# Windowed attention and a leaky-ReLU layer: the q and k casts of batches 4 to 7 go to GpSimd alone, and the list that orders the work counts transfers of later batches as landing later

## The chip, the cores and the metric

The kernel runs on one core of one Trainium2 chip. The metric is the device time of one execution in microseconds (us); the time before is the median of three runs. One further execution was recorded by the hardware profiler; all durations below come from that one. Engines are named as in the profile: PE is TensorE's matmul, PEld its weight load, DVE is VectorE, ACT is ScalarE, POOL is GpSimd, SP is SyncE, whose queue issues nearly all transfers.

## The reference

There are 8 batches of 8 heads with 576 positions of 64 numbers. Each query sees keys of a window only: heads 0 to 3 the last 32 positions, heads 4 to 7 every fourth of the last 128 ("dilated"). The result of attention, 4608 tokens of 512 numbers, goes through two matrices with a leaky ReLU between.

```python
scores = scale * np.matmul(q, k.transpose(0, 1, 3, 2))
rel = pos[:, None] - pos[None, :]
mask_plain = (rel >= 0) & (rel < window)                     # window 32
mask_dil = (rel >= 0) & (rel < window * dilation) & (rel % dilation == 0)   # dilation 4
attn = softmax of the scores under the head's mask
x = attn @ v, heads side by side                              # 4608 x 512
h = x @ w_in                                                  # 512 x 2048
out = np.maximum(0.01 * h, h) @ w_out                         # 2048 x 512
```

## The kernel before

**Two streams of work share the engines.** Attention is done batch by batch; within a batch it goes by pairs of heads, four visits in the order dilated, dilated, plain, plain. The layer is done in 12 chunks of 384 tokens, three for every two batches: `up` (L1012) is `w_in` times the attention's result `xt`, ACT applies the leaky ReLU and writes `gt` (L1023), and the products with `w_out` (L1065 and L1156) follow. From the fifth token tile on, four tiles are taken together in `group`, which replaces eight block products by seven (a Strassen scheme); the sums and differences this needs are DVE instructions at L1142, and the results are put together at L1185 (ACT or DVE) and L1193 (DVE).

**How q and k of batches 2 to 7 reach the scores.** For each half of a batch (two visits), SP issues four transfers of q and four of k into two `stg` buffers; there are four such buffers for this, so the two halves that follow each other use different ones. A cast from float32 to float16 takes one visit's q or k from `stg` to `nat` (three buffers): four casts of 128x576 per half, eight per batch, 48 in all. It shows as L287 on POOL and as L285 on ACT. DVE then transposes `nat` (L621, L636, L655); for the dilated heads POOL rearranges what DVE turned (L642, L649). The result is in `slots` (six of them), from which PE makes the scores (L949). ACT takes the exponential (L962), DVE multiplies by the mask (L965), PE sums and applies v (L955), ACT makes the reciprocal of the sum (L973, L976), DVE normalizes into `xt` (L984). v has its own casts on POOL (L287, `v_all<-vst`), four per batch.

**What sets the order.** Nothing is ordered on the chip: a list scheduler, `_Plan.run`, runs as Python while the program is built. Each task has costs on the engines that may do it, a latency, dependencies and a priority. The planner gives each engine its tasks in the order of its modelled start times, and where a task may run on several engines it takes the one that ends it soonest. On the chip every engine then works through its list in that order and waits at each instruction for what it needs. For a transfer the plan counts the time to issue it, its service time and then `1.1 + t.late`; `t.late` is `LATE` for the transfers of batches 2 to 7 and of the late masks, and less for those ahead:

```python
server = begin + t.service
t.done = server + 1.1 + t.late
```

The tasks that need the transfer are ready after `t.done` in the plan, and so are the loads that reuse the buffer when those tasks have ended. The number changes the order alone; no instruction waits for it on the chip. The modelled cost of a cast of n columns is `0.05 + n * 0.00102` us on POOL and `0.06 + n * 0.00087` us on ACT. Output stores stand in the same SP list as the loads.

Of the kernel before, what the change touches and what calls it, by code (L numbers as in the profile page):

```python
# [12 lines left out]
ALU = mybir.AluOpType  # L13

WIN = 32
AHEAD, LATE, HOLD = 5.0, 4.0, 5.0
WHEN = (-5.0, 15.0, 50.0, 77.0, 112.0, 138.0, 172.0, 200.0)
CON = -1484.5
AFTER = -1495.0
# [139 lines left out]
def kernel(  # L159
# [42 lines left out]
    def at(tl, p0, p1, off, *dims):  # L202

        row = tl.ap[0][0]
        return bass.AP(tensor=tl.tensor, offset=tl.offset + p0 * row + off,
                       ap=[[row, p1 - p0]] + [list(d) for d in dims])
# [73 lines left out]
    def cast(dst, src, n, deps, prio, engines=("POOL",)):  # L280
        cost = {"POOL": 0.05 + n * 0.00102, "DVE": 0.08 + n * 0.00056, "ACT": 0.06 + n * 0.00087}

        def fn(e):
            if e == "ACT":
                nc.scalar.copy(out=dst, in_=src)  # L285
            else:
                ENG[e].tensor_copy(out=dst, in_=src)  # L287
        return add(tuple((e, cost[e]) for e in engines), None, 0.2, deps, fn, prio, 0.0, "cast")
# [6 lines left out]
    def ring(name, n, users):  # L295

        r = rings.setdefault(name, [])
        waits = r[-n] if len(r) >= n else []
        r.append(users)
        return (len(r) - 1) % n, waits  # L300
# [43 lines left out]
    CENG = ("POOL", "DVE")  # L344
# [14 lines left out]
    def load_group(b, g, prio, prio_v):  # L359
# [3 lines left out]
        early = b < EARLY  # L363
# [64 lines left out]
        for j in range(2):  # L428
            nn, n_old = ring("NAT", NNAT, n_users := [])
            na, c_qk = nat[nn], []  # L430
            for o in range(2):
                st, s_users = stage[o]
                if early:
                    dst = at(na, 0, 128, o * 512, [D, 2], [128, 4], [1, D])
                    src = at(st, 0, 128, *((j * 512, [256, 2]) if first else (j * 256, [512, 2])), [D, 4], [1, D])
                    n = 512
                else:
                    dst, src, n = na[:, o * S:o * S + S], st[:, j * S:j * S + S], S
                c_qk.append(cast(dst, src, n, (loads[o][j:j + 1] if first else loads[o]) + n_old, prio,
                                 (("ACT",) if o else ("DVE",)) if first and dil and j == 0 else  # L440
                                 CENG if early else ("POOL", "ACT")))
                s_users.append(c_qk[-1])
            if not early:
                visits[b, 2 * g + j, 0] = (na, c_qk, n_users, vb[:, SLOT9 * j:SLOT9 * j + SLOT9],
                                           c_v, k_users)
                continue
            dn, d_old = ring("VD" if dil else "VP", NV, d_users := [])
            vt = (vd if dil else vp)[dn]
            n_v = 256 if dil else 384
            h_a, h_s = j * n_v, 2 * n_v  # L450
            n, w = n_v // D, 128 * (8 if dil else 6)
            c_v = [cast(at(vt, 0, 128, 0, [w, 2], [128, n], [1, D]),
                        at(vs, 0, 128, h_a, [h_s, 2], [D, n], [1, D]), 2 * n_v,
                        (lv if dil else lv[0] + lv[1]) + d_old, prio_v)]
            v_users += c_v
            seen_ones[b, 2 * g + j] = [t_ones["d" if dil else "p", dn]]
            kept[b, 2 * g + j] = vt, d_users
            visits[b, 2 * g + j, 0] = (na, c_qk, n_users, vt,
                                       c_v + ([t_one] if (b, 0) in TILED else
                                              [t_ones["d" if dil else "p", dn]]), d_users)  # L460
# [839 lines left out]
    def attend(b, part, first, step):  # L1300
        units = {None: (0, 1), 0: (0, 1), 1: (2,)}[part]
        if part is None and not late_mask:
            late_mask.append(load("SP", late_m, late_d, 128, 2 * NLATE, [], tick()))
        if part == 1:
            load_rest(b, ranks[b])
        for n, hp in enumerate((2, 3, 0, 1)):
            if part != 1 and n % 2 == 0:
                load_group(b, hp // 2, *(ranks[b, hp // 2, i] if b < EARLY else tick()
                                         for i in (0, 1)))
            got = turn(b, hp, part or 0, first + step * n)  # L1310
            for u in units:
                if part is None:
                    late_unit(b, hp, u, got, first + step * n)
                else:
                    unit(b, hp, part, u, got, first + step * n)
# [99 lines left out]
```

## Time and profile before

| what | value |
|---|---|
| time, median of 3 runs | 321.32 us (320.18 to 322.19) |
| the profiled execution: its time | 319.11 us |
| the profiled execution: its span, first to last instruction | 317.3 us |
| granted TensorE clock, mean | 0.999 |
| busy: PE, DVE, ACT, POOL | 297.9, 214.8, 202.9, 114.4 us |
| q and k casts 128x576 on POOL (L287) | 21, mean 727 ns |
| q and k casts 128x576 on ACT (L285) | 27, mean 674 ns |
| v casts 64x1152 on POOL (L287) | 24, mean 1235 ns |
| DVE transposes of `nat`, L621 and L636 | 24.0 and 17.4 us in all |
| POOL's waits for transfers of q and k / of v | 12.4 / 20.4 us |
| ACT's waits for transfers of q and k | 5.5 us |

The span is the time that the instructions cover; the 1.8 us between it and the execution's time lie around it. Busy times are sums over the whole span. An engine's wait is the idle time ahead of an instruction, put down to what came last; it costs time only where somebody waits for that engine in turn.

### The profile page before, as it was taken

The page shows a single profiled execution, that of the slowest core. Times are in us where ns is not written, and L with a number is a line of the kernel's source. Part 1 is how long each engine was busy: PE and PEld are TensorE (multiplying, and loading weights), DVE is VectorE, ACT ScalarE, POOL GpSimd, SP SyncE. Part 2 cuts the span into 40 slices and gives each one's busy share as a digit, 9 for nine tenths or more (in the row PEclk, how much of TensorE's full clock was granted, in tenths as well). Part 3 has the DMA queues.
Part 4 walks back from the last instruction along what each step waited for, and adds up shares of the span by engine and source line. Part 5 has one row for each costly group of instructions (what it writes and reads, how often), then busy time and mean ns, then how long its engine had stood idle before and what let it go on. Part 6 is the DMA issues. An engine that isn't in the chain of part 4 may idle for free.

```text
span 317.3 us, 7595 instructions
## 1 busy us (share of the span) xinstructions
PE 297.9 (94%) x2847; PEld 218.3 (69%) x2847; DVE 214.8 (68%) x422; ACT 202.9 (64%) x489; POOL 114.4 (36%) x156
## 2 busy tenths in 40 slices
PE   8868699899999999999997998999999999999985
PEld 3534365556988787787775876687877777767774
DVE  5786988975999989968868976886524341150172
ACT  3725464797898879587885876658565844454411
POOL 4479976259475166064508247120000000000000
PEclk9999999999999999999999999999999999999999
DMA  7999999689898996679859789612103010220223
GB/s 239 321 337 404 407 300 185 163 166 201 159 178 169 177 195 125 128 151 191 155 131 187 161 168 171 161 59 70 35 9 93 1 35 0 68 66 2 74 61 99
DMA packets 157300, 47.62 MB, mean 150 GB/s; under 512 B 137296, under 2 KB 154576, under 8 KB 157264
## 3 DMA queue, kind: packets, MB, share of 16 engines
q1 hardware_dynamic: 156688, 46.79, 62.2%
q8 instruction: 22, 0.36, 0.5%
q10 hardware_dynamic: 576, 0.35, 0.4%
q14 instruction: 14, 0.11, 0.1%
HBM read 37.68 MB, written 9.44 MB: 148 GB/s over the span
## 4 chain that ended last, share of the span: by engine, by line
PE 66%; DMA 7%; POOL 7%; SPq 5%; DVE 5%; ACT 4%; issue 4%; POOLq 0%; ACTq 0%; DVEq 0%
PE hps L1012 30%; PE fps L1156 19%; PE tp L1156 7%; SPq L277 5%; POOL w_in L287 4%; PE ops L955 3%; DMA wst<-in_moe_w_in_dram 3%; POOL v_all L287 2%; DMA stg<-in_q_dram 2%; PE fps L1065 2%; ACT gt L1023 2%; DVE slots L583 1%; DMA out_dram<-osb 1%; PE ops L1156 1%; DMA stg<-in_k_dram 1%
## 5 line engine op out<-in xcount | busy, mean ns | idle before, releaser
L1012 PE MATMUL hps<-xt,w_in 128*128 128x384 f16 (+1 forms) x812 | 146.7, 313 | 7.9 <-ACT gt L1023 3.3
L1023 ACT ACTIVATE gt<-hps 128x384 f16<-128x384 f32 (+1 forms) x203 | 93.3, 469 | 58.3 <-PE hps L1012 56.6
L1012 PEld LDWEIGHTS <-w_in 128*128 128x128 f16 x832 | 74.9, 98 | 43.8 <-issue 7.0
L1156 PEld LDWEIGHTS <-gt 128*128 128x128 f16 x768 | 73.1, 98 | 15.0 <-DVE gt L1142 2.0
L287 POOL CAST v_all<-vst 64x1152 f16<-64x1152 f32 (+3 forms) x36 | 39.8, 1111 | 26.1 <-DMA vst<-in_v_dram 20.4
L1156 PE MATMUL fps<-w_out,gt 128*128 128x256 f16 x368 | 47.5, 273 | 0.0
L984 DVE TENSOR_TENSOR xt<-ops,rc 128x288 f16<-128x288 f32 x48 | 26.8, 559 | 15.2 <-ACT rc L976 8.7
L965 DVE TENSOR_TENSOR ee<-ee,late_m 128x384 f16<-128x384 f16 (+1 forms) x48 | 22.8, 486 | 10.5 <-ACT ee L962 10.2
L1193 DVE TENSOR_TENSOR osb<-tp,stg 128x512 f32<-128x512 f32 x14 | 9.6, 687 | 27.1 <-ACT stg L1185 18.0
L621 DVE STREAM_TRANSPOSE slots<-nat 64x64 f16<-64x64 f16 (+1 forms) x48 | 24.0, 500 | 2.3 <-POOL nat L287 1.0
L287 POOL CAST nat<-stg 128x576 f16<-128x576 f32 (+1 forms) x24 | 17.0, 713 | 16.7 <-DMA stg<-in_q_dram 6.3
L285 ACT CAST nat<-stg 128x576 f16<-128x576 f32 (+1 forms) x28 | 18.5, 672 | 5.5 <-DMA stg<-in_q_dram 5.2
L1185 ACT COPY stg<-fps 128x512 f32<-128x512 f32 (+1 forms) x25 | 13.4, 535 | 12.9 <-PE fps L1156 12.7
L976 ACT ACTIVATE rc<-rc 128x288 f32<-128x288 f32 x48 | 21.3, 448 | 0.4
L642 POOL COPY slots<-turned 64x512 f16<-64x512 f16 x24 | 17.0, 710 | 10.3 <-DVE turned L636 9.5
L649 POOL COPY slots<-turned 128x576 f16<-128x576 f16 x12 | 8.7, 722 | 29.9 <-DVE turned L636 29.6
L636 DVE STREAM_TRANSPOSE turned<-nat 128x576 f16<-128x576 f16 (+1 forms) x24 | 17.4, 738 | 1.2 <-issue 0.9
L955 PEld LDWEIGHTS <-v_all 128*128 128x128 f16 x240 | 14.8, 98 | 3.4
L583 DVE COPY slots<-tp 64x128 f16<-64x128 f16 (+7 forms) x43 | 13.6, 333 | 4.5 <-PE tp L662 4.1
L1156 PE MATMUL fps<-wst,gt 128*128 128x256 f16 x128 | 16.4, 273 | 0.2 <-DVE gt L1142 0.2
L955 PE MATMUL ops<-ee,v_all 128*128 128x96 f16 (+2 forms) x240 | 16.4, 200 | 0.0
L1142 DVE TENSOR_TENSOR gt<-gt 128x1024 f16<-128x1024 f16 x21 | 15.0, 730 | 1.6 <-PE fps L1156 1.6
(113 smaller groups left out, 431.9 us busy)
## 6 DMA issues: line engine op xcount, KB each, us to landing
stg<-in_q_dram SPq DMA_DIRECT2D x48, 144.0 KB, 3.3
stg<-in_k_dram SPq DMA_DIRECT2D x48, 144.0 KB, 3.0
vst<-in_v_dram SPq DMA_DIRECT2D x12, 288.0 KB, 3.6
vst<-in_v_dram SPq DMA_DIRECT2D x24, 128.0 KB, 2.8
gt<-in_moe_w_in_dram SPq DMA_DIRECT2D x5, 512.0 KB, 8.0
xt<-in_moe_w_out_dram SPq DMA_DIRECT2D x3, 512.0 KB, 7.1
gt<-in_moe_w_out_dram SPq DMA_DIRECT2D x3, 512.0 KB
out_dram<-osb SPq DMA_DIRECT2D x12, 128.0 KB, 2.1
```

The lines of the kernel that those rows point to most:

```text
L285: nc.scalar.copy(out=dst, in_=src)
L287: ENG[e].tensor_copy(out=dst, in_=src)
L621: nc.vector.transpose(at(qb, p0, p0 + 64, p0 + c, *dims), na[p0:p0 + 64, S + c // 2:S + c // 2 + n])
L636: lambda e, xb=xb, o=o, n=n: nc.vector.transpose(xb[:, 0:n], na[:, o * S:o * S + n]),
L642: lambda e, xb=xb, p0=64 * h: ENG[e].tensor_copy(out=at(qb, p0, p0 + 64, p0, [128, 4], [512, 2], [1, 64]), in_=at(xb, p0, p0 + 64, 0, [1, ...
L955: nc.tensor.matmul(at(bk, 0, 128, o, *dims), stationary(s), et[:, c:c + n], start=i == 0, stop=i == len(parts) - 1, skip_group_check=True)
L965: lambda e: nc.vector.tensor_tensor(out=et[:, 0:w], in0=et[:, 0:w], in1=mk, op=ALU.mult), prio + 0.1)
L976: lambda e: nc.scalar.activation(out=rt[:, 0:NQ], in_=rt[:, 0:NQ], func=AF.Exp, scale=-1.0),
L984: lambda e: nc.vector.tensor_tensor(out=dst, in0=at(ot, 0, 128, 0, *src), in1=at(rt, 0, 128, 0, *src), op=ALU.mult), prio + 0.2)
L1012: nc.tensor.matmul(ht[:, 0:n], at(w_in, 0, 128, i * DFF + j // 2 * 256 + j % 2, [2, 128]), at(xt[m % 2], 0, 128, i * 1152 + x0 + x, [1, n] ...
L1023: lambda e: nc.scalar.activation(out=gt[c % NG][:, j * n_c + x:j * n_c + x + n], in_=ht[:, 0:n], func=AF.Prelu, alpha=0.01),
L1156: nc.tensor.matmul(bk[:, x:x + HN], tl[:, off + j * step:off + j * step + 128], rhs(j), start=first and x == 0 and j == 0, stop=j == HJ - ...
```

## The change

Two lines change. `LATE` goes from 4 to 7 us, and the q and k casts of batches 4 to 7 may run on POOL alone, where before the plan chose POOL or ACT for each. Batches 2 and 3 keep the choice, and batches 0 and 1 (`early`) are as they were. No instruction is added or taken away; the casts that ACT had for batches 4 to 7 become POOL's, and the whole list is made anew with the later landing times, so that the order may change on every engine from batch 2 on.

```diff
-AHEAD, LATE, HOLD = 5.0, 4.0, 5.0
+AHEAD, LATE, HOLD = 5.0, 7.0, 5.0
...
                 c_qk.append(cast(dst, src, n, (loads[o][j:j + 1] if first else loads[o]) + n_old, prio,
                                  (("ACT",) if o else ("DVE",)) if first and dil and j == 0 else
-                                 CENG if early else ("POOL", "ACT")))
+                                 CENG if early else ("POOL", "ACT") if b < 4 else ("POOL",)))
```

## The prediction

> **What bounds the kernel now.** I read the page's busy times and slices first, then the windows, PE's waits, and the timeline around each wait.
>
> ```profile
> PE 297.9 (94%) x2847; PEld 218.3 (69%) x2847; DVE 214.8 (68%) x422; ACT 202.9 (64%) x489; POOL 114.4 (36%) x156
> ...
> PE   8868699899999999999997998999999999999985
> ...
> POOL 4479976259475166064508247120000000000000
> ```
>
> PE is the bound: from the ninth slice on (63 us) it shows 9 except at the very end and in two slices in the middle, a 7 from 167 to 175 us and an 8 from 190 to 198 us, while the casts of batches 6 and 7 run. POOL is used for a third of the span and has nothing to do after 209 us. DVE is the second fullest. So the change can only win the time in which PE stands still, and only lose if it makes PE stand still elsewhere. The windows give the amounts:
>
> ```profile
> core 0: us, PE busy (x) PEld busy (x) DVE busy (x) ACT busy (x) POOL busy (x), PEclk, DMA share, GB/s
> ...
> 160.00:180.00 20.00, 18.39 (x200) 14.28 (x198) 16.66 (x29) 14.57 (x35) 9.83 (x11) 1.00 0.85 163
> 180.00:200.00 20.00, 19.12 (x178) 14.43 (x177) 13.62 (x23) 13.52 (x30) 9.62 (x12) 1.00 0.84 158
> ```
>
> PE's column falls short of 20 by 1.61 and 0.88 us. PE's own waits from 90 to 220 us name the engine:
>
> ```profile
> PE hps L1012 <- ACT gt L1023: 2.9, 3, 1.6
> PE sps L955 <- DVE ee L965: 0.4, 1, 0.4
> PE fps L1156 <- DVE gt L1142: 0.2, 1, 0.2
> ```
>
> An `up` waits because ACT has not emptied the bank it writes. Why ACT had not is in the timeline:
>
> ```profile
> 171.79 0.67 ACT L285 CAST nat<-stg 128x576 f16<-128x576 f32 x1 [2.14 <-DMA stg<-in_q_dram]
> ...
> 172.90 0.81 PE L1012 MATMUL hps<-xt,w_in 128*128 128x384 f16 x4 [1.61 <-ACT gt L1023]
> ...
> 194.97 0.67 ACT L285 CAST nat<-stg 128x576 f16<-128x576 f32 x1 [1.40 <-DMA stg<-in_q_dram]
> ...
> 196.09 1.46 PE L1012 MATMUL hps<-xt,w_in 128*128 128x384 f16 x8 [0.88 <-ACT gt L1023]
> ```
>
> Twice a q cast stands at the head of ACT's list before its transfer has landed, two ReLUs (L1023) stand behind it, and PE behind these: 1.61 + 0.88 = 2.49 us. The third wait on ACT (0.39 us at 104 us) follows two casts on ACT at 100.8 us; with the casts sorted by start, eight to a batch, these are the last two of batch 3, which the change leaves free to run on ACT.
>
> **The casts, part by part.** Sorted that way, batches 4 to 7 have 32 casts, 17 on ACT and 15 on POOL. A cast costs nearly the same on both:
>
> ```profile
> L287 POOL CAST nat<-stg 128x576 f16<-128x576 f32 x21 | 15.3, 727 | 15.0 <-DMA stg<-in_q_dram 6.3 <-DMA stg<-in_k_dram 4.5 <-ACT gt L1023 3.7
> L285 ACT CAST nat<-stg 128x576 f16<-128x576 f32 x27 | 17.9, 674 | 5.5 <-DMA stg<-in_q_dram 5.2 <-DMA stg<-in_k_dram 0.3
> ```
>
> Removed from ACT: 17 x 0.674 = 11.5 us of work and both waits above. ACT's work itself hid behind PE, so only the 2.49 us of waits count: **-2.49 us**. With the casts gone, what is late next is `nat`, and behind it only attention.
>
> Added to POOL: 17 x 0.727 = 12.4 us in some 100 us (103 to 200), where the five windows of 20 us from 100 on (two of them shown) have it busy for 10.69 + 7.03 + 9.98 + 9.83 + 9.62 = 47.2 us. It goes to about 60 of 100. The four casts of a half go one after another, 2.9 us, where two engines took 1.45: a visit's `nat` comes up to 1.5 us later. What hides this is the distance from POOL's last rearrangement of a dilated visit (L649) to that visit's first score (L949). In the timeline it is 110.46 to 119.87 and 120.37 to 127.3 us in batch 4 (less 0.7 for the row itself, 8.7 and 6.2 us of room), 157.7 to 185.8 in batch 6, 203.8 to 232.0 in batch 7. The smallest is four times the delay, so I take 0; without that cover it would be 1.5 us for each of 8 halves. Behind a waiting POOL cast now stand v casts and the L642/L649 copies, with the same room. The casts issue no transfers, and no DMA queue gains an entry.
>
> **The shared cost on DVE.** More POOL work lies beside DVE's:
>
> ```profile
> 165.53 0.69 DVE L1142 TENSOR_TENSOR pair<-gt 128x1024 f16<-128x1024 f16 x1 [0.19 <-ACT gt L1023]
> ...
> 168.81 1.15 POOL L287 CAST v_all<-vst 64x1152 f16<-64x1152 f32 x1 [0.70 <-DMA vst<-in_v_dram]
> 168.86 1.64 DVE L1142 TENSOR_TENSOR gt<-gt 128x1024 f16<-128x1024 f16 x1
> ```
>
> The same addition takes 0.69 us alone and 1.64 us beside a POOL cast. Over the trace, the rows of L1142 last 685 ns where no POOL row overlaps (50 of them) and 1014 where one covers over 60% (11); the masks of L965 go from 353 to 580 ns (384 wide) and 370 to 838 (416 wide). Transposes and L984 do not change. Excess now: 11 x 0.33 + 6 x 0.23 + 10 x 0.47 = 9.7 us of DVE time, next to some 75 us of POOL work from 60 to 209 us; 12.4 us more of it makes an estimated 1.6 us. DVE has 18.7 us idle from 100 to 200 us (its windows hold 18.35, 16.61, 16.08, 16.66 and 13.62), and with 9.7 us of excess PE waited 0.6 us for DVE, a share of 6% or 0.1 us of the 1.6. DVE gets fuller, so I take **+0.2 us**; the ends are 0 and 17 x 0.47 = 8.0 us (every moved cast hits a wide mask and PE pays all).
>
> The Trainium skill ("SBUF — State Buffer", Who interferes with whom) states for this that a VectorE instruction with two SBUF inputs and a GpSimd instruction that reads SBUF exclude each other, the later one standing still until the other ends. L1142 and L965 are of that kind, and the trace agrees in that they alone stretch. By that rule taken at its worst each moved cast blocks for its whole 0.67 us, 11.4 us in all; put in the place of the +0.2 us, it makes the sum a loss of 8.4 us instead of a gain.
>
> **LATE.** It moves no instruction by itself; it reorders. (a) Casts that stay on an engine's list come up to 3 us later in it, behind work that is ready; POOL's 12.4 us of waits for q and k shrink. (b) The 0.39 us at 104 us and 0.09 at 101 hang on two casts of batch 3 that keep the choice: half of it, **-0.24**. (c) In the SP list loads fall back against stores. One store stood behind loads until 196.0 us, and DVE's osb (L1193) waited 3.50 us for it, to 199.4; from there come the 0.19 and 0.37 us for which PE waited on DVE at 200 and 202 us. Half of that: **-0.28**. (d) Later landing in the plan frees `stg` later. In the trace the last cast from a buffer ends 4.8 us (batch 5's first q) to 17 us before its next load is issued, so 3 us do not lengthen the ring. (e) Attention may fall back by 3 us. Batch 3's last normalization ends at 121.95 us, chunk 4's first `up` runs at 124.26: 2.3 us of room, so up to 0.7 us lost; but its casts end 7 us before the scores, which go by PE's list. I take 0, with ends of -1.9 us (the gaps from 58 to 64 us close, where batch 2 starts) and +3.0 us (the shift goes straight through).
>
> **Sum.** -2.49 + 0.2 - 0.24 - 0.28 = -2.8 us, against the profiled execution's 319.11: 316.3. That execution was 2.2 us below the median of the runs, 321.32; moved over, **318.5 us**, 0.9% below.
>
> **Rivals.** First, *more is won*: the new order also closes the gaps from 58 to 64 us, 0.69 + 0.23 + 0.39 + 0.16 + 0.46 = 1.9 us. 318.5 - 1.9 = 316.6. For it: batch 2's transfers get the new number too. Against: the waits there are on v and on normalizations of batch 1. Second, *nothing is won*: the two places on ACT are filled with other work that waits, or the waits move to DVE, which stands at transposes for POOL's casts (it did so for 1.0 us in the whole trace); 321.3. Third, on the other side, *DVE becomes the bound*: POOL casts block masks and additions, place L965 and L1142 from 100 to 200 us. With all 8.0 us on the path and 2.49 gained it is 321.32 + 5.5 = 326.8. It decides where DVE has no room: from 100 to 120 us it has only 1.65 us, later 3.4 to 6.4 per 20 us. For it: DVE's 92% there. Against: that window has PE waiting 0.5 us only. The change also not doing what it says would be the second rival's time: the casts leave ACT in any order.
>
> **How the numbers follow.** Forecast 0.50, with its own range from 317 to 320: a little under half of it lies below 318.1, where it is faster by over 1% (about what a measurement of this kernel can tell from no change). More is won 0.20; nothing is won 0.06; DVE becomes the bound 0.24. Faster 0.22 + 0.20 = 0.42, same 0.28 + 0.06 = 0.34, slower 0.24. The range of 8 in 10 goes from 316.0, just below the second case, to 325.5: it holds the forecast, nothing won, and the lower part of the DVE case, and leaves the worst of it out.
>
> **What would show it.** Right: no L285 cast on ACT after batch 3, and no wait of ACT for q or k there; POOL busy near 127 us in all; PE's wait for ACT L1023 from 90 to 220 us under 0.6 us; windows from 160 to 200 us above 19.5 of 20. L1142 and L965 rows should be longer on the mean. Wrong: PE waits for DVE L965 or L1142, or for POOL's slots, of over 2 us, or a gap of PE ahead of chunk 4's first `up`.

## The result and the profile after

The changed kernel took 320.69 us (median, 318.26 to 323.24) against 322.06 us (320.18 to 323.11) for the kernel before, 12 executions each. The ratio is 0.9942, with a 95% interval from 0.9918 to 0.9965: faster by 0.6%, between 0.35 and 0.8%. A second comparison gave 319.17 against 321.43 us, ratio 0.9936 (0.9913 to 0.9960). The forecast was 0.9% faster.

The changed kernel was recorded three times: 323.24, 318.09 and 319.31 us. The first is a slow execution (over 1.5% above the fastest of its kernel) and the ratio leaves it out: its granted clock was 0.76 from 10 to 15 us, and its work from 60 us on started 2.8 us late. The lines below are from the second, of 318.09 us, span 316.3, which is the fastest of the three; where the other two differ, the text says so.

Its page, the same lines as before:

```profile
PE 299.0 (95%) x2847; PEld 218.6 (69%) x2847; DVE 215.7 (68%) x421; ACT 194.8 (62%) x472; POOL 127.5 (40%) x174
...
PE   7878799899989999999999999999999999999985
...
POOL 4479976239545858427814944360000000000000
```

The two digits under 9 in the middle of PE's line (7 and 8) are gone, but a new 8 stands in the twelfth slice (87 to 95 us). ACT has 17 instructions and 8 us less, POOL 13.1 us more, and POOL works until 210.5 us. The windows (PE, PEld, DVE, ACT, POOL busy, then clock and transfers):

```profile
100.00:120.00 20.00, 19.95 (x230) 15.95 (x228) 17.99 (x35) 15.76 (x41) 13.55 (x15) 1.00 0.98 177
120.00:140.00 20.00, 19.23 (x205) 14.71 (x203) 19.22 (x29) 13.10 (x33) 9.97 (x12) 1.00 0.60 126
...
160.00:180.00 20.00, 20.00 (x216) 15.44 (x214) 17.61 (x31) 14.67 (x38) 10.14 (x15) 1.00 0.85 168
180.00:200.00 20.00, 20.00 (x186) 15.26 (x185) 12.68 (x21) 11.20 (x26) 8.70 (x11) 1.00 0.87 163
```

From 160 to 200 us PE no longer stands still at all, where it lost 2.49 us. (From 180 to 200 us it is busy for 19.17 us in the third recording and 17.96 in the first.) But from 120 to 140, where it had been full, 0.77 us are lost, and DVE is busy there for 19.22 of 20. PE's waits from 90 to 220 us say the same:

```profile
PE ops L955 <- DVE xt L984: 0.9, 2, 0.8
PE sps L955 <- DVE ee L965: 0.6, 2, 0.3
PE hps L1012 <- ACT gt L1023: 0.5, 1, 0.5
```

The wait for ACT fell from 2.9 to 0.5 us; the wait for DVE rose from 0.6 to 1.5. In the third recording it is 2.9 us. PE's idle time from 90 to 220 us is 3.89 us in the first recording of the kernel before, and 4.90, 2.14 and 3.57 in the three of the kernel after. PE's gaps that are new stand at 89 to 94 and at 129 us (PE's timeline; the number in brackets is the gap ahead of the row):

```profile
89.13 0.82 PE L1012 MATMUL hps<-xt,w_in 128*128 128x192 f16 x8 [0.30 <-ACT gt L1023]
92.70 0.49 PE L1012 MATMUL hps<-xt,w_in 128*128 128x192 f16 x4 [0.47 <-ACT gt L1023]
93.96 0.35 PE L955 MATMUL sps<-ee,sides 128*128 128x96 f16 x5 [0.27 <-DVE ee L965]
130.16 0.33 PE L955 MATMUL ops<-ee,v_all 128*128 128x96 f16 x5 [0.77 <-DVE xt L984]
```

What DVE did when PE stood still at 129 us (DVE's and then POOL's timeline of the changed kernel; an entry of "x2" covers two instructions):

```profile
125.48 1.63 DVE L1142 TENSOR_TENSOR rest<-gt 128x1024 f16<-128x1024 f16 x1
127.03 1.63 DVE L1142 TENSOR_TENSOR pair<-gt 128x1024 f16<-128x1024 f16 x1
128.59 1.15 DVE L1142 TENSOR_TENSOR gt<-gt,gt 128x1024 f16<-128x1024 f16 x1
129.66 0.45 DVE L984 TENSOR_TENSOR xt<-ops,rc 128x288 f16<-128x288 f32 x1
```

```profile
125.30 2.81 POOL L287 CAST v_all<-vst 64x1152 f16<-64x1152 f32 x2
128.18 2.08 POOL L287 CAST nat<-stg 128x576 f16<-128x576 f32 x2
```

Three additions that take 0.69 us alone take 1.63, 1.63 and 1.15 beside POOL's casts; the normalization behind them, for which PE waits, ends an estimated 2.3 us later than it would (4.41 less 3 x 0.69). The gap at this place is 0.77 to 0.78 us in all three recordings.

### The profile page after: what moved, and what is told of

Same layout as the page of the kernel before. It is cut to its first block, busy times and chain, and to the rows that moved or that the text cites. A ratio compares the mean times of both kernels' runs of the same rounds, so it can differ in the third digit from the quotient of the medians.

```text
span 321.5 us, 7580 instructions
## 1 busy us (share of the span) xinstructions
PE 299.6 (93%) x2847; PEld 219.3 (68%) x2847; DVE 215.3 (67%) x421; ACT 194.7 (61%) x472; POOL 127.2 (40%) x174
## 4 chain that ended last, share of the span: by engine, by line
PE 61%; DVE 10%; DMA 10%; POOL 6%; SPq 6%; issue 4%; ACT 3%; DVEq 0%; POOLq 0%; ACTq 0%
PE hps L1012 26%; PE fps L1156 17%; PE tp L1156 6%; SPq L277 6%; POOL w_in L287 4%; DMA stg<-in_q_dram 4%; PE ops L955 3%; DMA wst<-in_moe_w_in_dram 3%; PE fps L1065 2%; DVE gt L1142 2%; DMA out_dram<-osb 2%; DMA vst<-in_v_dram 1%; ACT gt L1023 1%; DVE slots L583 1%; DVE xt L984 1%
## 5 line engine op out<-in xcount | busy, mean ns | idle before, releaser
L287 POOL CAST v_all<-vst 64x1152 f16<-64x1152 f32 (+3 forms) x36 | 39.0, 1090 | 19.5 <-DMA vst<-in_v_dram 15.2
L287 POOL CAST nat<-stg 128x576 f16<-128x576 f32 (+1 forms) x42 | 30.6, 748 | 9.5 <-DMA stg<-in_q_dram 5.8
L984 DVE TENSOR_TENSOR xt<-ops,rc 128x288 f16<-128x288 f32 x48 | 26.6, 555 | 10.8 <-ACT rc L976 6.5
L1193 DVE TENSOR_TENSOR osb<-tp,stg 128x512 f32<-128x512 f32 x14 | 9.7, 690 | 34.3 <-ACT stg L1185 20.1
L965 DVE TENSOR_TENSOR ee<-ee,late_m 128x384 f16<-128x384 f16 (+1 forms) x48 | 22.4, 485 | 10.4 <-ACT ee L962 10.3
L642 POOL COPY slots<-turned 64x512 f16<-64x512 f16 x24 | 16.1, 672 | 17.1 <-DVE turned L636 16.3
L649 POOL COPY slots<-turned 128x576 f16<-128x576 f16 x12 | 9.6, 800 | 30.0 <-DVE turned L636 29.8
L830 ACT ACTIVATE ee<-sps 128x384 f16<-128x384 f32 x20 | 9.8, 491 | 12.5 <-PE sps L824 9.9
L955 PEld LDWEIGHTS <-sides 128*128 128x128 f16 x240 | 13.2, 97 | 4.7 <-issue 2.9
L1142 DVE TENSOR_TENSOR gt<-gt 128x1024 f16<-128x1024 f16 x21 | 15.6, 754 | 1.3 <-PE fps L1156 1.3
```

What stands on the lines that cost most here:

```text
L955: nc.tensor.matmul(at(bk, 0, 128, o, *dims), stationary(s), et[:, c:c + n], start=i == 0, stop=i == len(parts) - 1, skip_group_check=True)
L965: lambda e: nc.vector.tensor_tensor(out=et[:, 0:w], in0=et[:, 0:w], in1=mk, op=ALU.mult), prio + 0.1)
L984: lambda e: nc.vector.tensor_tensor(out=dst, in0=at(ot, 0, 128, 0, *src), in1=at(rt, 0, 128, 0, *src), op=ALU.mult), prio + 0.2)
L1142: lambda e: ENG[e].tensor_tensor(out=dst, in0=a, in1=b, op=op),
```

## Experiments

Each kernel was timed in turn with the kernel before on the same chip, if nothing else is said. Theories are named by the letters of the expectations. "PE idle" is PE's idle time from 90 to 220 us in the kernel's own recording.

**The changed kernel again.** No edit.

> The changed kernel once more, for a profile that began undisturbed. Theory A (the two waits of ACT for q went away, new waits of PE for DVE took half of that back): 0.992 to 0.997 of the time before; from 90 to 220 us PE waits under 1 us for ACT at L1023 and 3 to 4 us for DVE (L965, L984), mostly behind DVE's wait for a store at about 190 and 204 us. Rival B (the gain comes from the early part, 40 to 90 us): PE idle from 40 to 90 us is over 1 us less than before, and what it loses after 90 us is as much as before.

Measured: 0.9936 (0.9913 to 0.9960); PE waited 0.5 us for ACT and 1.5 us for DVE; 40 to 90 us did not gain (PE idle 2.38 us, against 2.06 before: 20.00 - 19.26 + 30.00 - 28.36, against 20.00 - 19.31 + 30.00 - 28.63). The ratio and the wait for ACT are theory A's; its 3 to 4 us for DVE, mostly behind stores, did not come (1.5 us, and the one wait of DVE for a store, 2.06 us at 186 us, made no gap of PE). B falls.

**LATE alone.**

```diff
-AHEAD, LATE, HOLD = 5.0, 4.0, 5.0
+AHEAD, LATE, HOLD = 5.0, 7.0, 5.0
```

> LATE 7 with the casts on either engine as before. Theory A: casts stay on ACT but stand up to 3 us later in its list, which covers the 2.14 and 1.40 us by which the two q transfers came late; the waits of 1.61 and 0.88 us go, and without POOL's extra work DVE is not slowed: 0.990 to 0.995. Rival C (the engine is what counts): ACT waits again for some transfer and the ratio is 0.998 to 1.002. Rival D (any new order shifts the time by about a us either way): anywhere from 0.995 to 1.008 with other waits in its place.

Measured: 0.9932 (0.9905 to 0.9960), as much as both edits together. The casts stay on either engine (28 on ACT), no wait of ACT for q or k is left, and PE idle is 1.48 us. DVE's additions at the place of the gap:

```profile
127.78 0.68 DVE L1142 TENSOR_TENSOR rest<-gt 128x1024 f16<-128x1024 f16 x1
128.38 0.68 DVE L1142 TENSOR_TENSOR pair<-gt 128x1024 f16<-128x1024 f16 x1
128.98 0.68 DVE L1142 TENSOR_TENSOR gt<-gt,gt 128x1024 f16<-128x1024 f16 x1
```

POOL has nothing to do from 127.6 to 130.8 us there, the additions keep their 0.68 us, and the gap of 0.77 us is not there. Rival C (only the engine counts) falls.

**The engine alone.** LATE stays 4.

```diff
-                                 CENG if early else ("POOL", "ACT")))
+                                 CENG if early else ("POOL", "ACT") if b < 4 else ("POOL",)))
```

> Casts of batches 4 to 7 on POOL alone, LATE 4. Theory A: ACT's waits for q go all the same, POOL waits 12 us or more for transfers of q and k, DVE is slowed as in the changed kernel: 0.993 to 0.999. Rival E (LATE makes the gain): 1.000 or more, PE waiting for DVE that waits for POOL's late casts.

Measured: 0.9958 (0.9932 to 0.9984): faster, by 0.2 to 0.7%, and rival E's "1.000 or more" falls. But its recording, 321.0 us and so at the upper end of its executions (median 319.91), shows what LATE is for once the casts are on POOL:

```profile
166.89 1.28 POOL L287 CAST nat<-stg 128x576 f16<-128x576 f32 x2 [6.42 <-DMA stg<-in_k_dram]
```

```profile
167.60 0.49 DVE L621 STREAM_TRANSPOSE slots<-nat 64x64 f16<-64x64 f16 x2 [3.87 <-POOL nat L287]
```

POOL stands 6.42 us at a cast whose transfer is not there, DVE 3.87 us at the transpose behind that cast, and PE 2.48 us at a product behind a mask that stands behind the transpose. The wait has not gone; it has moved from ACT to POOL and DVE. So rival E's mechanism is there, though not its ratio. POOL's waits for q and k from 60 to 220 us are 15.4 us here, 10.8 before, and 7.0, 2.9 and 5.1 in the recordings of the changed kernel. The gap costs more than its 2.48 us in this recording: right behind it the granted clock is 0.70 (the number behind POOL's), and the 12 `up` products in this stretch take 449 ns on the mean, where the kernel before has 326:

```profile
170.00:175.00 5.00, 5.00 (x41) 3.31 (x40) 5.00 (x8) 2.39 (x6) 4.41 (x5) 0.70 1.21 192
```

**The engine alone, in the old order.** The list is made as before; then the casts of batches 4 to 7 go to POOL at the place they have.

```diff
 order = plan.run()
+for t in moved:          # the q and k casts of batches 4 to 7
+    t.eng = "POOL"
```

> The list is made as before (LATE 4, either engine) and then the casts of batches 4 to 7 that it gave to ACT are put on POOL at their place in the order; nothing else moves. Theory A: PE's waits of 1.61 and 0.88 us go, with no reordering to bring new ones but what POOL's 17 more casts cost DVE (0 to 1.6 us): 0.992 to 0.997. Rival D (reordering is what made the difference, not the engine): within 0.002 of the time before. Rival F (POOL's head of list waits for the transfers and holds up the L642 and L649 copies until DVE and PE wait): 1.005 or more.

Measured: 0.9979 (0.9952 to 1.0006). PE's gaps of 1.61 and 0.88 us behind ACT are gone, as theory A says, but PE idle is 4.37 us: gaps of 1.58 and 0.64 us behind normalizations and of 0.74 and 0.37 behind additions and masks have come. DVE waits 4.28 us at one transpose for a POOL cast that waited 6.21 us for k. So rival F's mechanism is real, and it eats the gain without making a loss. The ratio lies just outside theory A's range and rival D's, and its interval holds 1: in the old order the engine swap buys nothing that is clear of the noise.

**LATE 1 and LATE 10, casts on either engine.**

```diff
-AHEAD, LATE, HOLD = 5.0, 4.0, 5.0
+AHEAD, LATE, HOLD = 5.0, 1.0, 5.0      # and 10.0 in the second kernel
```

> LATE 1, casts on either engine. Theory A2 (the number works as a margin against transfers that land later than the list counts; 4 is too little, 7 enough): ACT and POOL stand longer ahead of casts, PE's waits behind them grow from 2.9 us to 5 us or more from 90 to 220 us: 1.006 to 1.02. Rival D (any new order shifts the time by about a us either way, the number's direction does not matter): 0.994 to 1.005, with ACT's waits for q and k no longer than the 5.5 us before.

> LATE 10, casts on either engine. Theory A2: ACT's waits for q and k are gone at 7 already, so nothing more is won: within 0.003 of what LATE 7 alone gave (0.9932), or slightly worse where attention falls back behind the chunks that need it. Rival G (more margin goes on winning): 0.990 or less. Rival D: back at 0.998 or more with other waits.

Measured: LATE 1 gives 1.0008 (0.9981 to 1.0036), LATE 10 gives 0.9961 (0.9936 to 0.9986). ACT's waits for q and k are 5.7 us at LATE 1, 5.5 (and 4.7 in another recording) at 4, and none at 7 and 10. So of the four values tried, 1 and 4 are alike and 7 and 10 are alike in this: theory A2's 1.006 for LATE 1 was wrong, and its statement on 10 (nothing more to win) was right. The ratio of LATE 1 is in rival D's range, which these two kernels do not rule out. At 10 the waits are elsewhere: PE idle 3.06 us, of it 1.47 us in one gap at 135 us behind DVE.

**ACT alone with LATE 7.**

```diff
-                                 CENG if early else ("POOL", "ACT")))
+                                 CENG if early else ("POOL", "ACT") if b < 4 else ("ACT",)))
```

> LATE 7 and the casts of batches 4 to 7 on ACT alone, the opposite of the change. Theory A2 (with the margin it does not matter which engine has the casts, as long as PE stays ahead of it): 0.991 to 0.997, ACT without waits of over 1 us for q or k, DVE some 2 us less busy from 90 to 220 us than in the changed kernel. Rival H (casts must leave ACT, as ACT's 0.67 us a cast delays the emptying of banks): 1.000 or more, PE waiting for ACT at L1023 for 3 us or more.

Measured: 0.9997 (0.9967 to 1.0026), outside theory A2's range, yet not by rival H's way: ACT has no wait for q or k, and PE waits only 0.5 us for ACT. PE waits 2.9 us for DVE instead: 0.93 us at 129 us and 1.56 at 201. With POOL freed, the planner gave POOL one of the additions of L1142, which takes 2.63 us there, and a mask of DVE beside it takes 1.69 us; just ahead of the gap at 201 us DVE had stood 2.65 us at L1193 for a store. DVE was not 2 us less busy but 0.6 more (110.54 us against 109.93 in the changed kernel). The expectation of theory A2 failed.

**The kernel before, recorded again.** No edit, one execution of 320.54 us.

> The kernel before once more, for a second profile. If its waits hang on when transfers land, they differ from execution to execution: theory A2 expects PE's idle time from 90 to 220 us between 3 and 7 us with the largest gap again behind a cast on ACT or a store that came late; the first profile, at 319.11 us, was some 2 us under the median, so more idle time than its 3.9 us is likelier. Rival: the same gaps at the same places within 0.2 us, and the difference between executions lies in the first 40 us.

Measured: PE idle 4.08 us, the largest gap at the same place and larger (ACT's row first, then PE's):

```profile
174.07 0.67 ACT L285 CAST nat<-stg 128x576 f16<-128x576 f32 x1 [3.22 <-DMA stg<-in_q_dram]
```

```profile
175.19 0.81 PE L1012 MATMUL hps<-xt,w_in 128*128 128x384 f16 x4 [2.69 <-ACT gt L1023]
```

ACT's wait is 3.22 us where it was 2.14, PE's 2.69 where it was 1.61. At the second place the gap is 0.15 us instead of 0.88. So these waits vary from one execution to the next; the sum was 2.49 and 2.84 us. Most of the difference arose in SP's list and not in the transfer: the last of the four q transfers took 2.71 us from issue to landing in the first recording and 2.87 here, but was issued 0.9 us later, counted from the gap near 59 us. What lies ahead varies too: a gap of 0.69 us that all recordings show near 59 us begins 1.2 us later here, at 59.97 us.

**HOLD 8.** In the changed kernel DVE's L1193 waits for stores. HOLD is the time after a store's landing that the list adds before an output buffer counts as free.

```diff
-AHEAD, LATE, HOLD = 5.0, 7.0, 5.0      # in the kernel before: 5.0, 4.0, 5.0
+AHEAD, LATE, HOLD = 5.0, 7.0, 8.0      # 5.0, 4.0, 8.0 in the third of these kernels
```

> The changed kernel with HOLD 8: the list counts an output buffer as free 3 us later after its store. Theory S (what took part of the gain back is DVE standing at L1193 for a store that SP issues late): DVE's waits for stores of 2.1 to 3.6 us near 190 and 200 us go, PE idles under 1.5 us from 90 to 220 us instead of 2.1, and the ratio is 0.988 to 0.992. Rival T (what took it back is DVE's masks and additions stretched beside POOL's casts, 0.8 us at 129 us): the waits for stores go but the ratio stays at 0.993 to 0.996. Rival D (any new order shifts the time by about a us): 0.997 or more.

> LATE 7 and HOLD 8, casts on either engine. Theory S: LATE alone already had no wait of DVE for a store in its profile, so HOLD adds little: 0.990 to 0.994. Rival D: 0.996 or more.

> The kernel before with HOLD 8 alone. Theory A (ACT's waits for late q transfers cost 2.5 to 2.8 us, the store at 196 us 0.6 us): the waits of ACT stay, 0.997 to 1.000. Rival D: beyond that on either side.

Measured: 1.0003 (0.9973 to 1.0034) for the changed kernel with HOLD 8, 1.0092 (1.0065 to 1.0119) for LATE 7 with HOLD 8 and casts on either engine, 1.0014 (0.9991 to 1.0038) for the kernel before with it. Theory S gave the place rightly and the remedy wrongly: DVE's waits for stores from 60 to 240 us grew, to 9.6 us in the first, where recordings of the changed kernel have 2.1 to 7.0. The second shows how one store can cost 5.63 us (DVE's row, then PE's):

```profile
205.79 0.69 DVE L1193 TENSOR_TENSOR osb<-fps,stg 128x512 f32<-128x512 f32 x1 [6.59 <-DMA out_dram<-osb]
```

```profile
210.36 1.87 PE L1156 MATMUL fps<-wst,rest 128*128 128x256 f16 x8 [5.63 <-DVE stg L1187]
```

SP issued v, q and k without a break from 185.93 to 200.75 us and stores only after that. All three ratios lie where rival D put them (the third just so: its interval reaches below theory A's 1.000, and ACT's waits stayed, at 4.2 us); the new order of LATE 7 cost 1.6% more than the same kernel without the new HOLD.

**The changed kernel, third recording.** No edit, one execution of 319.31 us.

> The changed kernel for a third profile. If its remaining waits hang on stores that land early or late, PE's idle time from 90 to 220 us lies between the 2.1 and 4 us of the other two, and the gap at about 129 us, which hangs on the order alone, is 0.8 us again.

Measured: PE idle 3.57 us; the gap at 129 us is 0.77 us again; gaps of 0.83 and 0.90 us at 188 and 202 us stand behind DVE's waits of 3.62 and 3.41 us for stores. Both as expected.

## Why the prediction was right or wrong

**-2.49 us, the two waits of ACT: right, and shown.** They are gone in each recording of the changed kernel, and in the kernels with LATE 7 or 10. But the prediction put this down to the engine, and that is only half of it. With LATE 4, the casts' leaving ACT takes ACT's waits away and hands the late transfer to POOL and DVE, where it cost PE 2.48 us in one gap with the list made anew, and 1.58 in the old order; with LATE 7 ACT has no such wait, whichever engine has the casts. The step that failed is "with the casts gone, what is late next is `nat`, and behind it only attention": behind `nat` stands DVE's list, in order, with masks, normalizations and additions that PE needs now. The room of 6 to 28 us ahead of the scores covers the data, not the engine that stands at it. In the changed kernel LATE 7 covers this step: its second and third recording have no wait of DVE at a transpose for a POOL cast (the first has 0.52 and 1.07 us). What took back part of the gain there is in the next two terms.

**+0.2 us for POOL's work on DVE: too small, though the work was not mis-sized.** The stretching of L1142 and L965 was foreseen, with 1.6 us of added DVE time. The rows' excess, over the prediction's times for rows alone, rose from 10.8 and 10.3 us (two recordings before) to 14.2 and 13.8 (second and third after), some 3.6 us more. Of it 0.77 us reached PE, over 20% where 6% was taken, at a place where DVE has no room (19.22 of 20 us busy). But it is the order more than POOL's amount of work that sets the excess. With the casts on POOL in the old order POOL is as busy from 60 to 220 us (88.4 us, the changed kernel 87.9, the kernel before 75.0), and the excess is 11.6, near what the prediction took; with the casts on ACT alone and LATE 7 POOL has 67.8 us and the excess is 15.2. The DVE rival named the condition, though for 100 to 120 us, and it came 20 us later. Its price of 8.0 us did not come near, nor did the worst case of 11.4. (The casts that left ACT were 18 and not 17, 27 before and 9 after; no term of the sum hangs on the one.)

**LATE's four terms.** (b) Half of the gap at 104 us was to go, -0.24. It went whole, but new gaps came at 89 to 94 us: PE's idle time from 85 to 105 us is 1.51 us against 0.88, +0.63, and it is 1.51 with LATE alone too, so it is LATE's; from 63 to 70 us it shrinks by 0.17. This is the second step that failed: the sum has no term for new gaps that the reordering brings. (c) Half of 0.56 us behind stores, -0.28: the gaps of this kind are 0.34 us in the second recording, behind a wait of DVE at L1193 that the profile puts down to ACT, and 1.73 in the third, behind stores; the order of SP's list did not cure this. (d) and (e): no sign of the ring or of a chunk waiting for attention in PE's gaps, as taken.

Added up for the second recording: -2.49 + 0.77 + 0.63 - 0.17 - 0.22 = -1.5 us. PE's idle time from 40 to 220 us has 4.52 us where it was 5.95, which is -1.4, and from the start of the gap near 59 us to the end of the span it has 257.2 us where the kernel before had 258.6. The prediction had -2.8. By the third recording, 258.8 us, next to nothing is won against 258.6 and 258.8, and the first has 259.9. So the range from 316.0 to 325.5 us held the measured 320.69, the forecast's own, 317 to 320, did not; the two timed medians fell by 1.4 and 2.3 us, half and four fifths of the forecast.

Of the signs that the prediction named, ACT's waits and POOL's 127.5 us came. The windows from 160 to 200 us were above 19.5 in the second recording alone, and the masks of 416 columns became shorter on the mean (564 to 492 ns), while the additions and the other masks became longer. A sign of being wrong, over 2 us of waits for DVE at L965 or L1142, came in the first recording (2.44 us at L965) and nearly in the third (2.0).

**What stays open.** Against the timed medians' 1.4 and 2.3 us, the second and third recording, counted from the gap near 59 us, show between 1.6 us won (257.2 against the 258.8 of the second recording before) and 0.3 lost. What lies ahead of that gap took from 58.6 to 61.6 us in the recordings, before and after alike, so single recordings can't settle half a per cent. The waits on transfers and stores differ between executions of one kernel, by a factor of 1.5 for ACT's wait in the kernel before, and which of them the timed executions had was not recorded. So it is shown that ACT's waits went and what came in their place; that their balance is the measured 0.6% was only argued.

It is clear that the waits' going is not enough: eight kernels have no cast on ACT that waits for a transfer, and their ratios go from 0.9932 to 1.0092. PE idle goes with the ratio in the main (1.48 us with 0.9932, 3.06 with 0.9961, 3.60 with 0.9997, 5.72 with 1.0003, 6.71 with 1.0092), so what a new order brings counts as much as what it removes, and that any new order shifts the time by a us or so (rival D) is not ruled out as the source of a part of the gain. POOL alone with LATE 4 does not fit that row (4.19 us with 0.9958). A part of this can be its recording, 1.1 us above the median: the stretch at a clock of 0.70 costs it an estimated 1.5 us (12 products, 449 less 326 ns each), and whether the other executions had the gap and the stretch is not known.

**The rivals.** More won in the early part: no, it lost 0.3 us from 40 to 90 us. Nothing won, with waits moved to DVE: this mechanism shows with LATE 4 and the casts on POOL; in the changed kernel DVE's waits at transposes are not what took back the gain. Slower by DVE: not with this order.

## What to carry to other kernels

Where instruction lists are fixed ahead, the head of a list that waits for a transfer costs whatever stands behind it on that engine; moving the waiting instruction to an idle engine helps only if the list of that engine, and of the engine that uses its result, has room. Putting it later in the list (a larger landing time in the plan) removed ACT's wait at no cost in instructions, and alone won as much as both edits together. It is no rule: the new order brings gaps of its own, and with the casts on ACT alone the same number won nothing. Judge such an edit by several executions and by the sum of PE's gaps, not by the one wait it aims at: of the reorderings tried here, the best won 0.7% and the worst lost 0.9%.

## What the runs showed of the hardware

A POOL cast can be held up by DVE, and not only the other way round. In the changed kernel a cast that takes 0.66 us alone took 2.82 us (106.33 to 109.15, the first of the two below; 2.82 us in the third recording too) while DVE ran additions and masks one after the other at their usual times:

```profile
106.33 3.43 POOL L287 CAST nat<-stg 128x576 f16<-128x576 f32 x2
```

```profile
106.22 0.66 DVE L1142 TENSOR_TENSOR gt<-gt,gt 128x1024 f16<-128x1024 f16 x1
106.82 0.34 DVE L965 TENSOR_TENSOR ee<-ee,late_m 128x384 f16<-128x384 f16 x1
107.08 0.68 DVE L1142 TENSOR_TENSOR gt<-pair,gt 128x1024 f16<-128x1024 f16 x1
107.68 0.34 DVE L965 TENSOR_TENSOR ee<-ee,late_m 128x384 f16<-128x384 f16 x1
107.95 0.68 DVE L1142 TENSOR_TENSOR gt<-gt 128x1024 f16<-128x1024 f16 x1
```

The Trainium skill ("SBUF — State Buffer", SBUF: two separate sides) says that whichever of the two starts first holds the shared port for its whole instruction and the other stands still. The trace agrees in kind, with more than one instruction's length: the cast ended only after DVE's run of five was over, at 108.6 us.

A gap of PE can be followed by a stretch at a lower clock. After 60 us four recordings have a gap of over 2 us: 2.48 us (POOL alone, LATE 4), 2.15 (the changed kernel with HOLD 8), 5.63 (LATE 7 with HOLD 8) and 2.69 (the kernel before, second recording). The granted clock was 0.70 from 170 to 175 us in the first, 0.66 from 205 to 210 in the second, 0.66 from 205 to 215 in the third, and 1.00 from 170 to 180 in the fourth, where nothing followed. No length from which the clock falls can be read from this: LATE 1 and LATE 10 have 0.69 and 0.66 from 60 to 65 us, behind gaps of under 1 us.
